# An attention-and-filter kernel on Trainium2: the filter's half-row products on VectorE, output sums partly from PSUM, and another list of batches

## The chip, the cores and the metric

One core of one Trainium2 chip runs the kernel. The metric is the device time of one execution in microseconds (us). Before the change three runs gave a median of 650.92 us (650.14 to 651.53).

The engines are named as in the profile: PE is TensorE's matrix product, PEld its weight load, DVE is VectorE, ACT is ScalarE, POOL is GpSimd, SP is SyncE, which here only issues DMA transfers. SBUF is the on-chip memory; PSUM is the small memory into which PE writes, in 8 banks of 128 partitions by 512 float32 numbers.

## The reference

Two unrelated parts share one launch, and their outputs stand side by side:

```python
S, D, H = 2048, 448, 16; Dh = D // H          # Dh = 28
# A: attention, 16 query heads, one head of keys and values
q = (x @ wq) as 16 heads;  k = x @ wk;  v = x @ wv
p = softmax(q @ k.T * Dh ** -0.5)
a = concat_heads(p @ v) @ wo                   # 2048 x 448
# B: a filter in the frequency domain
X = rfft2(x);  X = X * (w_r + 1j * w_i);  b = irfft2(X)   # 2048 x 448
out = concatenate([a, b], axis=-1)
```

The inputs are float32. The kernel splits an operand into a rounded part and a remainder where it needs float32 accuracy from a faster product: a cast (high part) and a subtraction (low part), both on DVE, and three products instead of one (`mm3`).

## The kernel before

**Attention.** Queries are cut into 4 blocks of 512 (c) and 4 groups of 4 heads (g): 16 pairs (c, g). Keys are cut into 16 blocks of 128. A *step* is one pair and one key block, 256 steps in all. In a step PE makes four score tiles of 128 x 512 (one for each head of the group, L875), each in a bank of its own; their exponentials go to SBUF; PE then multiplies them by the values (L830, eight instructions a step) into a bank that collects 16 steps.

**Batches.** Steps are gathered in batches of two, five or six: first all scores of the batch, then all products with V. The list `PLAN` (L47 to L52) writes each batch as a string. `-` is a score tile whose exponential ACT takes straight from PSUM (L819). `k` is a score tile that DVE copies to SBUF (L881), so that its bank is free early, and that ACT exponentiates later, two tiles in one instruction (L898). `e` is one that ACT takes at once. In batches of five or six the four `k` alternate with the first `-`. The last step of a batch waits in `kept`, and its product with V comes with the next batch. `spread` places the letters of other work among the scores:

- `A` and `B`: the first and second half of a filter unit (`fft2_a`, `fft2_b`), 16 of each,
- `W`: a quarter of the output projection of 128 rows (`wo_unit`), 48 pieces; `X` stands for `WWWW`,
- `Z`: the last stage of the filter (`fft3_a`, then `fft3_b`), 32 pieces; `Y` stands for `ZZ`.

**A filter unit.** `fft2_a(u)` multiplies 128 x 450 numbers by a transform, in three products into one bank (L557 to L559). DVE copies the bank to `us` (L602). POOL makes the two half-row products with the imaginary weights, `p2` from `us` and `wi` (L606, L607: 64 partitions each, crossing halves). DVE makes the product with the real weights, `pf` from `us` and `wr` (L610), splits the next unit's input (L588, L589), then adds the two products (L614) and splits the sum (L615, L616). `fft2_b(u)` multiplies that by the inverse transform, and DVE copies the result out (L628). wr and wi are loaded by DMAs that POOL issues (L575).

**An output quarter.** `fft3_b` makes four products into one bank (L672). DVE copies all of it (L676), then, out of the queue of deferred work, makes a sum and a difference of its halves in SBUF (L690, L683); POOL makes the last sum and difference (L684, L685), and SP stores the result.

**The order of work.** On PE, ACT and DVE the order is written out by the program itself. While it emits PE's instructions it keeps three clocks of planned time (`clock`), one for each engine. `put` queues deferred DVE work with a cost in nanoseconds (one cost for all operations of an entry), `passed` moves PE's clock and pops queued work while DVE's clock is behind, `need` pops until a named entry is done, and `at_once` charges DVE or ACT for work that is emitted on the spot. `take` hands out the bank that is planned to be free first, `give` returns one. `first=True` puts an entry in the queue that is served first. Other deferred DVE work is, for each pair (c, g): the preparation of the next pair's queries (`build_q`, L218, L220, L209, followed by nine DMAs on SP), and the normalisation of a finished pair (`norm`: transposition out of the bank L834, reciprocal L711, division L716, transposition L730, cast L731, subtraction L726, then moves of spare rows by SP and POOL, L700 and L703); and the splits of the slices of wo (`wo_split`, L551 to L554).

## Time and profile before

| | us |
|---|---|
| median of three runs | 650.92 |
| the profiled execution, whole time | 651.21 |
| the profiled execution, span of its instructions | 649.4 |
| PE busy | 639.5 |
| ACT busy | 552.6 |
| DVE busy | 386.4 |
| POOL busy | 121.1 |

A line of a group in the profile reads: line of the kernel, engine, operation, what it writes <- what it reads, shape, count, then busy time in us, mean duration of one in ns, and the idle time of the engine just before them with what ended it. A line of the timeline reads: start and duration in us, engine, line, operation, tiles, count, and in brackets idle time before it. A row of a table of stretches reads: the stretch in us from the start of the span, its length, busy time of PE, PEld, DVE, ACT and POOL with their counts of instructions, granted TensorE clock, share of the DMA engines, GB/s. Buffer numbers are left out of tile names: `s`, `sx` and `po` are banks.

### The profile page before, as it was taken

What the parts mean: (1) busy time and instruction counts of PE and PEld (TensorE: products, weight loads), DVE (VectorE), ACT (ScalarE), POOL (GpSimd) and SP (SyncE); (2) the same over time, 40 slices, a digit from 0 to 9 for tenths busy, and PEclk for the clock granted to TensorE, in tenths of its full rate; (3) what the DMA queues carried; (4) which work ended last, traced back from release to release, by engine and by line L of the source; (5) the groups of instructions that cost most, each with busy time, mean ns of one, the idle gap of its engine ahead of it and who ended that gap; (6) DMA issues with size and microseconds to landing.
All of it is one profiled execution on the core that took longest, in us unless ns stands there. A gap on an engine that the chain in (4) does not pass through costs nothing.

```text
span 649.4 us, 12044 instructions
## 1 busy us (share of the span) xinstructions
PE 639.5 (98%) x4470; PEld 381.7 (59%) x4470; DVE 386.4 (59%) x663; ACT 552.6 (85%) x1013; POOL 121.1 (19%) x182
## 2 busy tenths in 40 slices
PE   8999999999999999999999999999999999999996
PEld 6877655555454665556655565556655665556555
DVE  5999639999898957543753623164636422363631
ACT  5554999998989989888999898989998988989981
POOL 3022304344534221201130200003021100010110
PEclk9999999999999999999999999999999999999999
DMA  8765952443836251315042313013141403040001
GB/s 278 256 165 167 270 131 76 123 124 98 210 78 153 64 130 56 88 32 149 21 114 75 83 46 94 16 47 101 41 131 47 98 15 95 28 100 12 30 31 60
DMA packets 36114, 63.83 MB, mean 98 GB/s; under 512 B 7905, under 2 KB 23922, under 8 KB 35084
## 3 DMA queue, kind: packets, MB, share of 16 engines
q1 hardware_dynamic: 30832, 49.60, 27.7%
q0 software_dynamic: 4640, 12.48, 7.3%
q8 instruction: 36, 0.59, 0.4%
q10 hardware_dynamic: 576, 0.92, 0.4%
q14 instruction: 30, 0.25, 0.1%
HBM read 30.04 MB, written 14.75 MB: 69 GB/s over the span
## 4 chain that ended last, share of the span: by engine, by line
PE 90%; DVE 7%; DMA 1%; ACT 1%; issue 1%; SPq 0%; ACTq 0%; DVEq 0%
PE s L875 28%; PE s L830 22%; PE po L830 6%; PE s L343 6%; PE sx L875 4%; PE po L875 4%; PE s L739 3%; PE sx L830 3%; PE s L141 2%; PE s L672 2%; PE s L658 1%; PE sx L739 1%; PE po L739 1%; DVE bh L588 1%; PE pbb L160 1%; DVE k L881 1%
## 5 line engine op out<-in xcount | busy, mean ns | idle before, releaser
L819 ACT ACTIVATE p<-s 128x512 f32<-128x512 f32 x645 | 344.6, 631 | 40.4 <-PE s L875 33.4
L875 PE MATMUL s<-qa,ka 128*128 128x512 f32 x786 | 238.3, 408 | 2.1 <-DVE k L881 2.1
L875 PEld LDWEIGHTS s<-qa,ka 128*128 128x128 f32 x786 | 144.4, 188 | 76.3 <-issue 30.5
L830 PE MATMUL s<-p,vs 128*32 128x512 f32 x1136 | 134.1, 595 | 0.0
L881 DVE COPY k<-s 128x512 f32<-128x512 f32 x122 | 78.1, 680 | 75.9 <-PE s L875 75.7
L898 ACT ACTIVATE k<-k 128x1024 f32<-128x1024 f32 x86 | 88.1, 1103 | 0.0
L830 PEld LDWEIGHTS s<-p,vs 128*32 128x32 f32 x1136 | 34.4, 109 | 75.1 <-issue 72.2
L819 ACT ACTIVATE p<-sx 128x512 f32<-128x512 f32 x95 | 59.9, 630 | 4.1 <-PE sx L875 3.1
L819 ACT ACTIVATE p<-po 128x512 f32<-128x512 f32 x88 | 55.8, 634 | 6.4 <-PE po L875 4.7
L875 PE MATMUL sx<-qa,ka 128*128 128x512 f32 x121 | 48.8, 403 | 0.0
L703 POOL DMA_DIRECT2D ol<-ol x36 | 18.1, 510 | 161.7 <-DVE ol L726 72.8
L875 PE MATMUL po<-qa,ka 128*128 128x512 f32 x117 | 47.4, 405 | 0.0
L606 POOL TENSOR_TENSOR pwi<-us,wi 64x450 f32<-64x450 f32 x16 | 23.2, 1448 | 113.3 <-DVE us L602 76.3
L881 DVE COPY k<-po 128x512 f32<-128x512 f32 x27 | 18.4, 681 | 41.2 <-PE po L875 41.2
L830 PE MATMUL po<-p,vs 128*32 128x512 f32 x312 | 37.2, 595 | 0.0
L684 POOL TENSOR_TENSOR yo<-y 128x226 f32<-128x226 f32 x16 | 9.8, 610 | 145.5 <-DVE y L683 72.3
L830 PE MATMUL s<-k,vs 128*32 128x512 f32 x272 | 35.6, 594 | 0.0
L834 DVE STREAM_TRANSPOSE osb<-s 128x512 f32<-128x512 f32 x11 | 7.9, 715 | 38.8 <-PE s L830 38.8
L875 PEld LDWEIGHTS po<-qa,ka 128*128 128x128 f32 x117 | 22.0, 188 | 10.2 <-issue 3.4
L875 PEld LDWEIGHTS sx<-qa,ka 128*128 128x128 f32 x121 | 22.7, 188 | 8.3 <-issue 3.4
L830 PE MATMUL sx<-p,vs 128*32 128x512 f32 x208 | 24.8, 595 | 0.0
L881 DVE COPY k<-sx 128x512 f32<-128x512 f32 x23 | 15.6, 680 | 14.1 <-PE sx L875 14.0
(220 smaller groups left out, 841.1 us busy)
## 6 DMA issues: line engine op xcount, KB each, us to landing
qa<-qa SPq DMA_DIRECT2D x15, 512.0 KB
raw<-xa SPq DMA_DIRECT2D x16, 256.0 KB
xb<-xb SPq DMA_DIRECT2D x8, 512.0 KB
qa<-qh SPq DMA_DIRECT2D x64, 64.0 KB
qa<-ql SPq DMA_DIRECT2D x60, 64.0 KB
ob<-yo SPq DMA_DIRECT2D x16, 226.0 KB
t<-bs SPq DMA_DIRECT2D x16, 225.0 KB
wr<-wr POOLq DMA_DIRECT2D x16, 225.0 KB, 5.1
```

The source lines that it names most:

```text
L141: mm(pa[r0:r0 + 32, e, o0:o0 + n], f[:, 2 * r + k, 2 * p + e, h], cs1[:, 2 * r + k, :n], start=True, stop=True)
L343: mm(pq, w[:, j, gs], x[:, j], start=(j == 0 and n == 0), stop=(j == 3 and n == 1))
L606: nc.gpsimd.tensor_tensor(p2[0:64], us[64:128], wi[64:128], op=ALU.mult)
L672: mm(py[:, k], z[:w, r, js], cs3[:w, k], start=True, stop=True)
L684: nc.gpsimd.tensor_tensor(yo[:, 0:2], y1[:, 0], y1[:, 1], op=ALU.add)
L703: nc.gpsimd.dma_start(ol[c][o, g].bitcast(F32), ol[c][r, 0].bitcast(F32))
L739: mm(p, x[c][:, g, s], w, start=(g == 0 and n == 0), stop=(g == NG - 1 and n == 2))
L819: nc.scalar.activation(tiles[-1][:, h % 2], sc, AF.Exp, scale=SCALE)
L830: mm(po[c, g][32 * i:32 * i + 32], vs[:, kc], ps[i // 2][:, i % 2], start=(n == 1), stop=(n == 16))
L875: begun.append(mm(sc, ka[:, kc * 128:(kc + 1) * 128], qa[c, g][:, h], start=True, stop=True))
L881: nc.vector.tensor_copy(keep[h // 2][:, h % 2], sc)
L898: nc.scalar.activation(p, p, AF.Exp, scale=SCALE)
```

## The change

- `fft2_a`: the copy to `us` goes. DVE makes all three products straight from the bank, the two half-row products first. The sum and its split (`pr`) are queued ahead of the next unit's split, which followed the real product before.
- `fft3_b`: DVE copies half of the bank's columns and makes the sum and the difference from the other half in PSUM and this copy, at once; POOL's two operations and the store follow without a queue.
- The list of batches: until step 65 it is the same. Then units A and B stay in batches of five for longer, the four pieces of a projection always stand together (`X`), some together with A and B (`BAX`, `XBB`), and a plain batch of five precedes the first Z. It has 50 batches instead of 49, and 176 tiles `k` instead of 172.
- `put` takes a cost for each operation. The loads and splits of wo are placed anew.

```diff
--- before.py
+++ after.py
@@ -45,11 +45,10 @@
 
 
 PLAN = ["eeeeF", "eeee"] + 4 * [spread(2, "", 0)]
-PLAN += ["-k-k-k-k----------A--"] + [spread(5, u) for u in ["A"] + 9 * ["BA"]]
-PLAN += [spread(6, u) for u in ["BA"] + 4 * ["WBWA"] + 2 * ["WBW"] + ["X"]]
-PLAN += [spread(6, u) for u in 5 * ["Y"] + 4 * ["X"] + 6 * ["Y"] + 4 * ["X"]]
-left = (256 - sum(k in "-ke" for b in PLAN for k in b) // 4)
-PLAN += [spread(6, "Y")] * (left // 6) + [spread(left % 6, "Y")] * (left % 6 > 0)
+FIVE, SIX = spread(5, "BA"), {u: spread(6, u) for u in ("X", "Y", "BAX", "XBB")}
+PLAN += [spread(5, "A", 4, 1.6), spread(5, "A")] + 11 * [FIVE] + [SIX["X"], FIVE, SIX["X"], SIX["BAX"], FIVE]
+PLAN += [SIX["XBB"], spread(5, "")]
+PLAN += 4 * [SIX["Y"]] + 4 * [SIX["X"]] + 7 * [SIX["Y"]] + 4 * [SIX["X"]] + 3 * [SIX["Y"]] + 2 * [spread(5, "Y")]
 
 
 WARM = 10, 10
@@ -215,12 +214,12 @@
                     behind(mv, stored[-1])
             nc.sync.dma_start(q[64:128].bitcast(F32), q[0:64].bitcast(F32))
 
-        ops = [lambda: nc.vector.tensor_scalar(qt, qraw[:, g, cs], mask, cvec[:, g, c:c + 1],
-                                               op0=ALU.mult, op1=ALU.add),
-               lambda: nc.vector.tensor_copy(qh, qt), split]
+        ops = [(540, lambda: nc.vector.tensor_scalar(qt, qraw[:, g, cs], mask, cvec[:, g, c:c + 1],
+                                                     op0=ALU.mult, op1=ALU.add)),
+               (450, lambda: nc.vector.tensor_copy(qh, qt)), (710, split)]
         if not first:
             return ops
-        for op in ops:
+        for _, op in ops:
             op()
         return q, qh, ql
 
@@ -506,11 +505,11 @@
     ap = pools.enter_context(tc.tile_pool(name="ap", bufs=2))
     pp = pools.enter_context(tc.tile_pool(name="pp", bufs=P_BUFS))
 
-    queue, done = (deque(), deque()), {("y", -1), ("pr", -1)}
-
-    def put(key, ops, work=528, first=False):
-
-        for i, op in enumerate(ops):
+    queue, done = (deque(), deque()), {("pr", -1)}
+
+    def put(key, ops, first=False):
+
+        for i, (work, op) in enumerate(ops):
             queue[not first].append(((key if i + 1 == len(ops) else None), op, work))
 
     def pop():
@@ -548,10 +547,10 @@
     def wo_split(g):
         w = wo[g]
         if g >= NG:
-            put(("wo", g), [lambda: nc.vector.tensor_copy(wox[:, g - NG], w)])
+            put(("wo", g), [(400, lambda: nc.vector.tensor_copy(wox[:, g - NG], w))])
             return
-        put(("wo", g), [lambda: nc.vector.tensor_copy(woh[:, g], w),
-                        lambda: nc.vector.tensor_tensor(wol[:, g], w, woh[:, g].bitcast(F32), op=ALU.subtract)])
+        put(("wo", g), [(400, lambda: nc.vector.tensor_copy(woh[:, g], w)), (630, lambda: nc.vector.tensor_tensor(
+            wol[:, g], w, woh[:, g].bitcast(F32), op=ALU.subtract))])
 
     def mm3(out, w, h, l):
         mm(out, fc[w + "h"], h, start=True, stop=False)
@@ -585,8 +584,8 @@
         b = b2["b", q][:, 2 * v:2 * v + 2]
         bh = b2["h", u] = fp.tile([128, 2, DF], F32R, name="bh", bufs=1)
         put(("split", u), [
-            lambda: nc.vector.tensor_copy(bh, b.bitcast(F32)),
-            lambda: nc.vector.tensor_tensor(b, b.bitcast(F32), bh.bitcast(F32), op=ALU.subtract)], first=True)
+            (400, lambda: nc.vector.tensor_copy(bh, b.bitcast(F32))),
+            (630, lambda: nc.vector.tensor_tensor(b, b.bitcast(F32), bh.bitcast(F32), op=ALU.subtract))], True)
 
     def fft2_a(u):
         q, v = divmod(u, 2)
@@ -598,22 +597,20 @@
         pu = halves2(bank)
         mm3(pu, "g1", b2["h", u], b)
         passed(608)
-        us = fp.tile([128, 2, DF], F32, name="us", tag="us", bufs=1)
-        nc.vector.tensor_copy(us, pu)
-        at_once(600)
+        pf, p2 = fp.tile([128, 2, DF], F32, name="pwr"), fp.tile([128, 2, DF], F32, name="pwi")
+        nc.vector.tensor_tensor(p2[0:64], pu[64:128], wi[64:128], op=ALU.mult)
+        nc.vector.tensor_tensor(p2[64:128], pu[0:64], wi[0:64], op=ALU.mult)
+        nc.vector.tensor_tensor(pf, pu, wr, op=ALU.mult)
+        at_once(1800)
         give(bank)
-        pf, p2 = fp.tile([128, 2, DF], F32, name="pwr"), fp.tile([128, 2, DF], F32, name="pwi")
-        nc.gpsimd.tensor_tensor(p2[0:64], us[64:128], wi[64:128], op=ALU.mult)
-        nc.gpsimd.tensor_tensor(p2[64:128], us[0:64], wi[0:64], op=ALU.mult)
         h = fp.tile([128, 2, DF], F32R, name="ph")
         p = fp.tile([128, 2, DF], F32R, name="pl")
-        put(("half", u), [lambda: nc.vector.tensor_tensor(pf, us, wr, op=ALU.mult)], first=True)
+        put(("pr", u), [
+            (700, lambda: nc.vector.scalar_tensor_tensor(pf, p2, sgn, pf, op0=ALU.mult, op1=ALU.add)),
+            (420, lambda: nc.vector.tensor_copy(h, pf)),
+            (640, lambda: nc.vector.tensor_tensor(p, pf, h.bitcast(F32), op=ALU.subtract))], True)
         if u < 15:
             fft2_split(u + 1)
-        put(("pr", u), [
-            lambda: nc.vector.scalar_tensor_tensor(pf, p2, sgn, pf, op0=ALU.mult, op1=ALU.add),
-            lambda: nc.vector.tensor_copy(h, pf),
-            lambda: nc.vector.tensor_tensor(p, pf, h.bitcast(F32), op=ALU.subtract)], first=True)
         pr[u] = h, p
 
     def fft2_b(u):
@@ -671,23 +668,18 @@
         for k, (z, w, r) in enumerate(((ze, 113, 0), (zo, 112, 0), (zo, 112, 1), (ze, 113, 1))):
             mm(py[:, k], z[:w, r, js], cs3[:w, k], start=True, stop=True)
         passed(888)
-        need(("y", 2 * q + v - 1))
-        m = fp.tile([128, 4, 113], F32, name="m", tag="us", bufs=1)
-        nc.vector.tensor_copy(m, py)
-        at_once()
+        y1 = fp.tile([128, 2, 2, 113], F32, name="y1", tag="pwr")
+        m = fp.tile([128, 2, 113], F32, name="m", tag="us", bufs=1)
+        nc.vector.tensor_copy(m, py[:, 2:4])
+        nc.vector.tensor_tensor(y1[:, :, 0], py[:, 0:2], m, op=ALU.add)
+        nc.vector.tensor_tensor(y1[:, :, 1], py[:, 0:2], m, op=ALU.subtract)
+        at_once(1100)
         give(bank)
-        y1 = fp.tile([128, 2, 2, 113], F32, name="y1", tag="pwr")
         yo = fp.tile([128, 4, 113], F32, name="yo", tag="pwi")
-
-        def sums():
-            nc.vector.tensor_tensor(y1[:, :, 1], m[:, 0:2], m[:, 2:4], op=ALU.subtract)
-            nc.gpsimd.tensor_tensor(yo[:, 0:2], y1[:, 0], y1[:, 1], op=ALU.add)
-            nc.gpsimd.tensor_tensor(yo[:, 2:4], y1[:, 0], y1[:, 1], op=ALU.subtract)
-            r0 = (2 * q + v) * 128
-            nc.sync.dma_start(t["ob"][r0:r0 + 128], yo)
-
-        put(("y", 2 * q + v), [
-            lambda: nc.vector.tensor_tensor(y1[:, :, 0], m[:, 0:2], m[:, 2:4], op=ALU.add), sums], 300)
+        nc.gpsimd.tensor_tensor(yo[:, 0:2], y1[:, 0], y1[:, 1], op=ALU.add)
+        nc.gpsimd.tensor_tensor(yo[:, 2:4], y1[:, 0], y1[:, 1], op=ALU.subtract)
+        r0 = (2 * q + v) * 128
+        nc.sync.dma_start(t["ob"][r0:r0 + 128], yo)
 
 
     oh, ol, osb = {}, {}, {}
@@ -727,8 +719,8 @@
             if c < NC - 1:
                 spares(c, g)
 
-        put(("o", c, g), [lambda: divide(c, g), lambda: nc.vector.transpose(o, o),
-                          lambda: nc.vector.tensor_copy(h, o), rest], 640)
+        put(("o", c, g), [(960, lambda: divide(c, g)), (710, lambda: nc.vector.transpose(o, o)),
+                          (430, lambda: nc.vector.tensor_copy(h, o)), (690, rest)])
 
     def wo_mm(p, c, k, gs):
         s = slice(k * 128, k * 128 + 128)
@@ -793,8 +785,8 @@
         if u % 2 == 0 and u < 14:
             at(step - 1, fft2_load, u // 2 + 1)
     for g in range(2 * NG - 1):
-        at(where["B"][g + 2] - 6, wo_load, g)
-        at(where["B"][g + 2], wo_split, g)
+        at(where["B"][g + 1] - 4, wo_load, g)
+        at(where["B"][g + 1] + 4, wo_split, g)
     for q in range(8):
         at(max(where["Z"][4 * q] - 8, where["B"][-1] + 1), fft3_load, q)
 
@@ -847,7 +839,7 @@
         for f, a in later.pop(step, []):
             f(*a)
         if step % 16 == 3 and step < 240:
-            put(("q", step // 16 + 1), build_q(*order[step // 16 + 1]), first=True)
+            put(("q", step // 16 + 1), build_q(*order[step // 16 + 1]), True)
         while norms and step > waits_for_output(norms[0][0]):
             norm(*norms.popleft())
```

## The prediction

> **What bounds the kernel now.** I read the page first, then a table of stretches by batch, then the timeline of VectorE inside two batches.
>
> ```profile
> span 649.4 us, 12044 instructions
> PE 639.5 (98%) x4470; PEld 381.7 (59%) x4470; DVE 386.4 (59%) x663; ACT 552.6 (85%) x1013; POOL 121.1 (19%) x182
> PE 90%; DVE 7%; DMA 1%; ACT 1%; issue 1%; SPq 0%; ACTq 0%; DVEq 0%
> ```
>
> TensorE (PE) sets the time, and the change takes no product from it. What can move is the time in which PE waits. The chain of waits goes through VectorE (DVE) for 7% although DVE is busy 59% of the span: DVE must be late in one stage. The next table shows which. The edges of its stretches are the starts of the products with V (L830) of consecutive batches, as the timeline has them, so each row but the second is one batch of five steps (the first holds one filter unit, the others two) (columns: stretch, its length, busy time of PE, PEld, DVE, ACT, POOL, then clock and DMA). The second row is nine batches in one.
>
> ```profile
> 96.31:106.34 10.03, 10.03 (x64) 5.44 (x64) 9.39 (x14) 9.48 (x19) 4.37 (x4) 1.00 0.08 20
> 106.34:206.71 100.37, 97.43 (x596) 53.51 (x595) 91.59 (x146) 90.30 (x164) 41.18 (x54) 1.00 0.54 138
> 128.50:139.15 10.65, 10.65 (x68) 6.00 (x67) 9.20 (x15) 9.95 (x20) 5.09 (x8) 1.00 0.74 197
> 139.15:150.97 11.82, 10.96 (x67) 5.84 (x66) 11.58 (x19) 9.97 (x20) 3.28 (x4) 1.00 0.16 56
> 173.08:184.01 10.93, 10.91 (x67) 5.92 (x66) 10.67 (x18) 10.04 (x20) 5.08 (x8) 1.00 0.56 151
> 184.01:196.06 12.05, 10.91 (x67) 5.93 (x67) 11.48 (x19) 10.01 (x20) 5.57 (x8) 1.00 0.37 81
> ```
>
> Batches of the same work take 10.65 to 12.05 us, and the long ones are those in which DVE is full (11.58 of 11.82, 11.48 of 12.05). Nine at the shortest length would be 9 x 10.65 = 95.85 us, so 100.37 - 95.85 = 4.52 us are waits. ACT has 9.95 of 10.65 and isn't the limit. The shortest and the longest batch differ so:
>
> ```profile
> 127.38 0.63 DVE L602 COPY us<-s 128x450 f32<-128x450 f32 x1 [0.95 <-PE s L559]
> ...
> 133.70 1.29 DVE L881 COPY k<-s 128x512 f32<-128x512 f32 x2 [0.92 <-PE s L875]
> ```
> ```profile
> 182.90 0.63 DVE L602 COPY us<-s 128x450 f32<-128x450 f32 x1
> 183.44 0.68 DVE L209 TENSOR_TENSOR ql<-ql,qh 128x512 fp32r<-128x512 f32 x1
> 184.04 1.58 DVE L610 TENSOR_TENSOR pwr<-us,wr 128x450 f32<-128x450 f32 x1
> 185.55 1.34 DVE L588 CAST bh<-b 128x450 fp32r<-128x450 f32 x1
> 186.93 0.63 DVE L589 TENSOR_TENSOR b<-b,bh 128x450 fp32r<-128x450 f32 x1
> 187.47 0.68 DVE L614 SCALAR_TENSOR_TENSOR pwr<-pwi,sgn,pwr 128x450 f32<-128x450 f32 x1
> 188.19 0.40 DVE L615 CAST ph<-pwr 128x450 fp32r<-128x450 f32 x1
> 188.62 0.63 DVE L616 TENSOR_TENSOR pl<-pwr,ph 128x450 fp32r<-128x450 f32 x1
> 189.16 0.70 DVE L730 STREAM_TRANSPOSE osb<-osb 128x512 f32<-128x512 f32 x1
> 189.90 0.43 DVE L731 CAST oh<-osb 128x512 fp32r<-128x512 f32 x1
> 190.36 0.69 DVE L726 TENSOR_TENSOR ol<-osb,oh 128x512 fp32r<-128x512 f32 x1
> 190.97 0.68 DVE L881 COPY k<-s 128x512 f32<-128x512 f32 x1
> ...
> 192.17 1.28 DVE L881 COPY k<-s 128x512 f32<-128x512 f32 x2
> ```
> ```profile
> 191.71 0.50 PE L875 MATMUL s<-qa,ka 128*128 128x512 f32 x1 [1.14 <-DVE k L881]
> ```
>
> From the copy that empties the filter's bank (us) to the next score copy (k) pass 6.32 us in the short batch, where k then waits for PE itself (0.92 us idle), and 190.97 - 182.90 = 8.07 us in the long one, where PE waits for k. The long batch is 12.05 - 10.65 = 1.40 us over, so about 8.07 - 1.40 = **6.67 us is what PE gives DVE** between these points; what DVE needs beyond is lost. The durations add up to 8.4 us for the 8.07 us (neighbours overlap a little), so a sum of durations is slightly too high.
>
> **The filter's products (lines 601 to 617).** Two copies of the same kind stand in that list at very different prices: L588 1.34 us, L615 0.40 us, both 128x450 casts. The groups over the nine batches say why:
>
> ```profile
> L588 DVE CAST bh<-b 128x450 fp32r<-128x450 f32 x9 | 10.4, 1159 | 0.0
> L589 DVE TENSOR_TENSOR b<-b,bh 128x450 fp32r<-128x450 f32 x9 | 10.0, 1106 | 0.3
> L610 DVE TENSOR_TENSOR pwr<-us,wr 128x450 f32<-128x450 f32 x9 | 7.4, 821 | 0.2
> L606 POOL TENSOR_TENSOR pwi<-us,wi 64x450 f32<-64x450 f32 x10 | 14.6, 1463 | 50.1 <-DVE us L602 43.3 <-DMA b<-t 6.8
> L607 POOL TENSOR_TENSOR pwi<-us,wi 64x450 f32<-64x450 f32 x9 | 10.3, 1150 | 0.6
> ```
>
> After us, POOL multiplies the two half-rows for 1.46 + 1.15 = 2.6 us, and just then DVE runs L610, L588 and L589, which stretch from 0.63, 0.40 and 0.63 (the shortest row of the same shape in the list above) to 0.82, 1.16 and 1.11. Before, a unit costs DVE 0.63 (us) + 0.82 + 1.16 + 1.11 + 0.68 + 0.40 + 0.63 = 5.43 us. After, there is no us and POOL multiplies nothing in this stage, so the rest returns to its undisturbed price: three products + 0.40 + 0.63 + 0.68 + 0.40 + 0.63 = three products + 2.74.
>
> No row shows a two-operand product that reads PSUM. Below, it can't beat the 0.40 us of the plain cast from SBUF; above I take the 1.16 us of the disturbed cast. Nearest are the copy out of PSUM of the same 450 columns (us, 0.63) and the two-operand L616 (0.63); the half-row products have half the partitions but all 450 columns. I take 0.63, so 1.89 + 2.74 = 4.63 us, 0.8 us less than before.
>
> In the changed program the order on DVE between these products and the next k copy holds, beside those 4.63 us, at most: L209, the transposition and the cast of an output (0.68 + 0.70 + 0.43, together 6.44 us); transposition, cast and subtraction (1.82, 6.45); or the splits of two slices of wo (each a cast and a subtraction like L615 and L616, 2 x 1.03, 6.69 us). All of the eleven groups up to step 75 are at or under the 6.67 us. So nearly the whole 4.52 us go; I keep 0.3 for uneven edges: **-4.2 us**.
>
> [...]
>
> What is moved with it: the bank is held for three products instead of one copy, 1.3 us more. In the changed order its next taker is a score of the following batch, behind all products with V, so these cover it; were the cover gone, a score would wait up to 1.3 us in each batch. A product that waits for wr or wi now stops DVE and the k copies behind it; the loads are issued ten steps ahead, and on POOL's queue nothing but DMA issues stands before them. The q moves on SP keep their place, 13 steps before use.
>
> **The output quarters (fft3_b) and the stores.**
>
> ```profile
> L676 DVE COPY m<-s 128x452 f32<-128x452 f32 x11 | 6.9, 628 | 3.4 <-PE s L672 2.6
> L690 DVE TENSOR_TENSOR y<-m 128x226 f32<-128x226 f32 x16 | 8.1, 505 | 1.2
> ```
>
> Before: a copy (0.63) and two sums at up to 0.51. After: a copy of half the columns (between 0.31 and 0.63) and two sums straight from PSUM at about 0.5, so 1.3 to 1.6 us for 1.65, but all three hold the bank. It is next taken five scores later or more, and DVE is half idle in this stage (rows below): nothing, against up to 0.7 us for each of 16 quarters if the bank were wanted at once. The sums on POOL and the store on SP are now issued at once; behind the store on SP stand q moves and the next quarter's loads, needed a batch later.
>
> **The list of batches.** From the end of the nine batches to the last products with V:
>
> ```profile
> 206.71:628.32 421.61, 421.61 (x2717) 245.52 (x2716) 211.66 (x357) 381.28 (x702) 54.12 (x84) 1.00 0.25 66
> 206.71:300.08 93.37, 93.37 (x567) 53.33 (x566) 61.85 (x94) 83.42 (x155) 19.24 (x20) 1.00 0.29 75
> 339.27:352.18 12.91, 12.91 (x90) 7.63 (x89) 3.93 (x7) 11.96 (x24) 1.65 (x3) 1.00 0.36 98
> 352.18:365.65 13.47, 13.47 (x89) 7.63 (x88) 9.11 (x17) 12.48 (x25) 1.10 (x3) 1.00 0.14 34
> 391.98:405.40 13.42, 13.42 (x84) 7.90 (x83) 3.82 (x6) 11.99 (x24) 0.00 (x0) 1.00 0.41 96
> 616.33:628.32 11.99, 11.99 (x85) 6.92 (x84) 4.82 (x9) 10.54 (x21) 1.08 (x2) 1.00 0.01 1
> ```
>
> Prices of whole batches without waits: five steps with A and B 10.65; with one filter unit 10.03, so a unit is 0.62 and five plain steps 9.41; six steps with four projection pieces (X) 13.42, so BAX and XBB are 13.42 + 1.24 = 14.66; six with two Z (Y) 12.91. The last row is a five behind a six, and so holds one more step of products with V than a five of its own; such a step of eight instructions takes 0.86 us from start to start:
>
> ```profile
> 353.06 1.04 PE L830 MATMUL s<-k,vs 128*32 128x512 f32 x8
> 353.92 1.04 PE L830 MATMUL s<-p,vs 128*32 128x512 f32 x8
> ```
>
> A five with two Z is thus 11.13. From step 65 on, after: 4 x 10.65 + 2 x 13.42 + 2 x 14.66 + 9.41 + 14 x 12.91 + 8 x 13.42 + 2 x 11.13 = **418.6 us** for the same 191 steps, against 421.61: **-3.0 us**. It holds one batch more than before (50 for 49 in all), which costs its change to and from the products with V. What it saves: the 0.56 us of the batch at 352.18 (DVE does an output's division before its k copies there, and two later batches start at the same place in their 16 steps; in the new list none does), and the waits of the stretch to 300.08, in which a projection's bank stays taken over two batches; in one piece it is held for four pieces only. I keep 0.7 back: the first X needs spare rows that are moved only just before it, and the plain five gives ACT no rest.
>
> **Sum.** -4.2 - 3.0 + 0.7 = -6.5 us. The profiled execution took 651.21 us around its span of 649.4; the median of the three runs is 650.92, 0.3 lower. 651.21 - 6.5 = 644.7, from the median 644.4; I say **644.6 us**. Start-up, first filter unit and the final projections are unchanged.
>
> **The rivals.** (1) *The products from PSUM are dear.* At 1.16 us each, the disturbed cast's price, a unit is 3.48 + 2.74 = 6.22 us; with up to 2.06 of other work the groups overrun 6.67 by 0.3 to 1.6 us, by my count 11 us in twelve batches: 650.9 + 11 - 4.5 - 3.0 = 654.4, slower. It decides from about 1.05 us per product. For it: an unseen operation, and twice the reads of PSUM. Against: both nearest rows say 0.63. (2) *DVE stays late in this stage*, since the planner fills the room it has won with other work (the q parts, the splits of wo) ahead of k: then the list alone pays, 650.9 - 3.0 = 647.9. Against it stands the order of the changed program. (3) *The list is no gain*: X in one piece, with its six or more waits for an output's rows, gives back 3 us: 650.9 - 4.2 = 646.7. (4) *Nothing arrives*: (2) and (3) together, 650.9; the waits then come from somewhere that neither part touches, such as ACT at 9.95 of 10.65.
>
> **Chances.** Forecast (643 to 646.5) 0.62; (3) 0.12; (2) 0.10; (4) 0.05; (1) 0.11. The likeliest's own range is 643.2 to 646.5: the lower end is no waits at all (650.9 - 7.5 = 643.4), the upper products of 0.82 us (L610), which cost the fullest groups 1.8 us. The 8-in-10 range is 643.0 to 650.0: it leaves out (1) and most of (4). A change under 0.2% (1.3 us) can't be told from none here. Faster 0.84, same 0.05, slower 0.11.
>
> **What would show it.** Right: every five-step batch between 96 and 210 us at 10.6 to 10.8 us; L588's successor at 0.40 us and L589's at 0.63; three products near 0.63; no idle time of PE put down to a k copy; no batch of Y over 13.1. Wrong: products over 0.9 us; k copies still late with DVE full; PE waiting in the first X batch for oh; more idle time of PE behind ACT in the batches of five.

## The result, and the profile after

The kernel after takes 646.94 us in the median of four runs (646.39 to 647.73), the kernel before 651.2 beside it: ratio 0.9938, 95% interval 0.9921 to 0.9956. In five more runs it took 646.62 (0.9937, 0.9923 to 0.995). The profiled execution took 646.39 us. Its page (span, busy time of the engines, the chain that ended last by engine):

```profile
span 644.5 us, 12021 instructions
PE 639.0 (99%) x4470; PEld 381.5 (59%) x4470; DVE 370.6 (58%) x683; ACT 552.6 (86%) x1011; POOL 79.9 (12%) x150
PE 96%; DMA 1%; DVE 1%; SPq 1%; issue 0%; ACT 0%; ACTq 0%; DVEq 0%
```

PE has 96% of the chain that ended last instead of 90, DVE 1% instead of 7: the late k copies are gone. The view of who waited for whom shows the same. These are the waits that it lists for PE between the batches of two and the tail, first before, then after (us in total, times, longest):

```profile
PE s L875 <- DVE k L881: 2.1, 3, 1.1
PE s L557 <- DVE k L881: 0.9, 1, 0.9
```
```profile
PE s L867 <- DMA qa<-qa: 0.2, 1, 0.2
```

The groups of DVE over the nine batches of five show what the products cost now:

```profile
L609 DVE SCALAR_TENSOR_TENSOR pwr<-pwi,sgn,pwr 128x450 f32<-128x450 f32 x9 | 6.2, 687 | 0.2
L588 DVE TENSOR_TENSOR b<-b,bh 128x450 fp32r<-128x450 f32 x9 | 5.6, 623 | 0.3
L601 DVE TENSOR_TENSOR pwi<-s,wi 64x450 f32<-64x450 f32 x8 | 5.0, 629 | 3.6 <-PE s L558 1.8 <-ACT p L811 1.7
L602 DVE TENSOR_TENSOR pwi<-s,wi 64x450 f32<-64x450 f32 x8 | 5.0, 621 | 0.2
L603 DVE TENSOR_TENSOR pwr<-s,wr 128x450 f32<-128x450 f32 x7 | 4.4, 627 | 0.1
L587 DVE CAST bh<-b 128x450 fp32r<-128x450 f32 x9 | 3.5, 390 | 0.0
```

Products 0.62 to 0.63 us, the cast 0.39 for 1.16, the subtraction 0.62 for 1.11.

For the time by stage I cut each span at the starts of products with V: at the last batch of two, at the batch of steps 60 to 64 (the end of the nine fives), and at the last batch. Stretch M1 lies between the first two, M2 between the last two, T from there to the end of the span. Ahead of M1 no code is changed; its length was 88.44 us in the profile of before, 87.01 and 87.37 in the two of after, and 87.3 to 88.2 in the others, and the order of instructions on DVE and ACT is the same there, so that 1.4 us of the difference of the two spans (4.9) belong to the execution and not to the change. A batch *loses* what it takes beyond the time of its own work on PE.

| kernel | median us | ratio, 95% interval | M1 | M2 | T |
|---|---|---|---|---|---|
| before | 650.7 to 651.2 | | 118.27 | 421.62 | 21.11 |
| after | 646.94 | 0.9938 (0.9921 to 0.9956) | 115.15 | 422.33 | 20.04 |
| after again (r1_again) | 646.62 | 0.9937 (0.9923 to 0.995) | 114.80 | 422.45 | 20.03 |
| e1_products_alone | 649.21 | 0.9974 (0.9962 to 0.9985) | 114.86 | 423.49 | 21.21 |
| e2_old_quarters | 647.62 | 0.9949 (0.9935 to 0.9962) | 114.86 | 423.18 | 20.02 |
| e3_old_list | 648.02 | 0.9954 (0.9941 to 0.9968) | 114.80 | 422.15 | 21.13 |
| e4_list_alone | 651.2 | 1.0005 (0.9996 to 1.0015) | 118.33 | 423.22 | 20.04 |
| e5_idle_products | 647.6, one run | | 115.60 | 422.76 | 20.03 |
| e6_copy_first | 651.53, one run | | 114.42 | 426.35 | 21.17 |
| e7_two_more_on_act | 646.73 | 0.9938 (0.9921 to 0.9954) | 114.79 | 422.06 | 20.02 |
| e8_third_list | 647.38 | 0.9943 (0.993 to 0.9956) | 114.80 | 420.73 | 21.89 |
| e9_q_earlier | 645.89 | 0.9925 (0.991 to 0.994) | 115.08 | 421.25 | 20.02 |
| e10_flat_costs | 647.78 | 0.9947 (0.9935 to 0.9959) | 116.83 | 421.84 | 20.01 |
| e11_together | 647.75 | 0.995 (0.9936 to 0.9964) | 115.09 | 419.78 | 22.95 |

M1 fell by 3.1 to 3.5 us, M2 rose by 0.7 to 0.8, T fell by 1.1. M1 and T repeat to 0.4 and 0.1 us where nothing in them differs, M2 to about 0.4. (e8 and e11 end with a batch of six: 0.86 us, a step of products with V, has moved from M2 to T.) The stretches that matter, after (the second row is the nine batches of five, the fourth is M2):

```profile
94.91:105.42 10.51, 10.51 (x65) 5.43 (x64) 8.83 (x16) 9.94 (x19) 0.11 (x1) 1.00 0.00 1
105.42:202.16 96.74, 96.64 (x595) 54.00 (x595) 85.04 (x154) 89.43 (x164) 18.22 (x35) 1.00 0.56 143
202.16:624.49 422.33, 422.13 (x2717) 245.27 (x2716) 204.01 (x368) 381.39 (x700) 39.75 (x73) 1.00 0.25 66
223.37:236.65 13.28, 13.08 (x76) 7.68 (x76) 7.06 (x13) 11.54 (x23) 2.00 (x4) 1.00 0.39 99
248.02:260.59 12.57, 12.57 (x76) 7.67 (x75) 8.10 (x15) 11.60 (x23) 0.59 (x1) 1.00 0.30 82
301.18:312.07 10.89, 10.89 (x70) 5.09 (x69) 5.55 (x10) 9.45 (x19) 3.15 (x6) 1.00 0.48 136
337.31:350.19 12.88, 12.88 (x89) 7.61 (x88) 3.87 (x6) 11.94 (x24) 0.49 (x1) 1.00 0.26 76
350.19:363.36 13.17, 13.17 (x89) 7.49 (x89) 8.30 (x18) 12.23 (x24) 1.74 (x4) 1.00 0.22 55
```

The nine fives take 96.74 us (96.39 in the second profile) for 100.37. The batch ahead of them takes 10.51 for 10.03. Further on, two batches of the same work (six steps with X) take 13.28 and 12.57, two of Y 13.17 and 12.88. Below, a batch is named by its first step: the 13.28 is batch 75, the 10.51 batch 15.

### The profile page after: what moved, and what is told of

Read it like the earlier page. It is cut to its first block, busy times and chain, and to the rows that moved or that the text cites. A ratio compares the mean times of both kernels' runs of the same rounds, so it can differ in the third digit from the quotient of the medians.

```text
span 644.5 us, 12021 instructions
## 1 busy us (share of the span) xinstructions
PE 639.0 (99%) x4470; PEld 381.5 (59%) x4470; DVE 370.6 (58%) x683; ACT 552.6 (86%) x1011; POOL 79.9 (12%) x150
## 4 chain that ended last, share of the span: by engine, by line
PE 96%; DMA 1%; DVE 1%; SPq 1%; issue 0%; ACT 0%; ACTq 0%; DVEq 0%
PE s L867 30%; PE s L822 23%; PE po L822 7%; PE s L342 6%; PE sx L867 5%; PE sx L822 4%; PE po L867 4%; PE s L731 4%; PE s L140 2%; PE s L655 2%; PE s L669 2%; PE po L731 1%; PE pbb L159 1%; DMA qa<-qa 1%; PE s L290 1%; PE s L558 1%
## 5 line engine op out<-in xcount | busy, mean ns | idle before, releaser
L811 ACT ACTIVATE p<-s 128x512 f32<-128x512 f32 x632 | 340.1, 627 | 37.1 <-PE s L867 31.4
L873 DVE COPY k<-s 128x512 f32<-128x512 f32 x131 | 84.1, 683 | 125.4 <-PE s L867 125.4
L890 ACT ACTIVATE k<-k 128x1024 f32<-128x1024 f32 x88 | 90.3, 1108 | 0.0
L811 ACT ACTIVATE p<-sx 128x512 f32<-128x512 f32 x109 | 68.3, 626 | 7.0 <-PE sx L867 6.4
L811 ACT ACTIVATE p<-po 128x512 f32<-128x512 f32 x83 | 52.8, 636 | 4.8 <-PE po L867 2.3
L867 PE MATMUL sx<-qa,ka 128*128 128x512 f32 x130 | 53.2, 409 | 0.0
L867 PE MATMUL po<-qa,ka 128*128 128x512 f32 x112 | 45.2, 403 | 0.0
L822 PE MATMUL s<-k,vs 128*32 128x512 f32 x296 | 38.7, 594 | 0.0
L867 PEld LDWEIGHTS po<-qa,ka 128*128 128x128 f32 x112 | 21.1, 188 | 7.6 <-issue 2.5
L822 PEld LDWEIGHTS po<-p,vs 128*32 128x32 f32 x328 | 9.8, 110 | 21.9 <-issue 21.3
L342 PE MATMUL s<-xh,wqh 128*128 128x512 f32 x56 | 22.7, 404 | 0.0
```

Source lines behind the costliest of these rows:

```text
L342: mm(pq, w[:, j, gs], x[:, j], start=(j == 0 and n == 0), stop=(j == 3 and n == 1))
L811: nc.scalar.activation(tiles[-1][:, h % 2], sc, AF.Exp, scale=SCALE)
L822: mm(po[c, g][32 * i:32 * i + 32], vs[:, kc], ps[i // 2][:, i % 2], start=(n == 1), stop=(n == 16))
L867: begun.append(mm(sc, ka[:, kc * 128:(kc + 1) * 128], qa[c, g][:, h], start=True, stop=True))
L873: nc.vector.tensor_copy(keep[h // 2][:, h % 2], sc)
L890: nc.scalar.activation(p, p, AF.Exp, scale=SCALE)
```

## The experiments

**The parts alone.** Four kernels, each with one or two parts of the change: r1_again is the kernel after once more. e3_old_list takes back the list and the due steps of wo; e2_old_quarters takes back `fft3_b`; e1_products_alone takes back both, so that `fft2_a` and the costs for each operation are left:

```diff
# e3 and e1, from after
-PLAN += [spread(5, "A", 4, 1.6), spread(5, "A")] + 11 * [FIVE] + [SIX["X"], FIVE, SIX["X"], SIX["BAX"], FIVE]
...
+PLAN += ["-k-k-k-k----------A--"] + [spread(5, u) for u in ["A"] + 9 * ["BA"]]
...
-        at(where["B"][g + 1] - 4, wo_load, g)
-        at(where["B"][g + 1] + 4, wo_split, g)
+        at(where["B"][g + 2] - 6, wo_load, g)
+        at(where["B"][g + 2], wo_split, g)
# e2 and e1, from after
-        nc.vector.tensor_copy(m, py[:, 2:4])
-        nc.vector.tensor_tensor(y1[:, :, 0], py[:, 0:2], m, op=ALU.add)
...
+        nc.vector.tensor_copy(m, py)
+        at_once()
...
```

> The changed kernel once more, to separate what belongs to the program from what differs between executions. 'The middle' below is the stretch from the first products with V of the last two-step batch to those of the last batch: 88.44 to 628.32 = 539.88 us before, 87.01 to 624.49 = 537.48 us in the first profile after. If the middle belongs to the program, it is 537.3 to 537.7 again, and only the stretches before and after it (1.43 and 1.07 us shorter in the first profile after) move. The rival: the middle itself varies by a microsecond or more between executions; then single profiles can't divide the change.

> Of the change only the filter's products (all three on VectorE from PSUM, with the costs per operation); the old list of batches and the old output quarters. Theory 1 (the products pay, the list pays nothing): the five-step batches fall to 10.7 us, the middle to 535.6 to 536.4 us, at least as fast as the whole change. Theory 2 (the products and the list each pay part, as forecast): the middle is about 536.3 and the whole change would be faster, which its 537.48 already speaks against. Theory 3 (the shift of work to VectorE only pays in the new list): the middle stays at 539 or more.

> The changed kernel with the old output quarters (whole bank copied, sums from SBUF out of the queue). Theory A (the new quarters cost, because the bank is held for three operations instead of one and VectorE ends later before the next scores): the Y batches with quarters get shorter, the middle by 0.5 to 1.5 us, 536.0 to 537.0. Rival, as forecast (the quarters cost nothing): the middle within 0.3 us of 537.48.

> The changed kernel with the old list of batches and the old places of the loads and splits of wo. Theory 1: no slower than the whole change, middle 536.0 to 537.0. Theory 2: slower than the whole change by up to 3 us, middle 538.5 to 540.5.

Measured: M1 is the same in all four (114.80 to 114.86), so the products with their costs make all of its gain. From before to e1 M2 *grows* by 1.87 us; from e1 to e3 (the quarters) it falls by 1.34; from e3 to after (the list) it rises by 0.2 to 0.3, while T falls by 1.1. With the old quarters the same list takes 0.3 off M2 (e1 to e2), so either way it is within what M2 repeats to. The medians say the same: 1.7 for the products and costs, 1.2 for the quarters, and 1.1 to 1.4 for the list, which is what T gave. So the quarters are worth 0.7 to 1.3 us, the list nothing in the stage for which it was made. Not all of this was expected: M1 and M2 together are 538.35 us in e1, which none of its three theories gave, and 538.04 in e2, more than either of its two allowed. In r1 (537.25) and e3 (536.96, theory 1's stretch) they are as expected.

The quarters show in the batches with an output's division. In the new list these are 132, 180 and 228: they take 13.43, 13.43 and 13.42 us with the old quarters (e2) and 13.17, 13.25 and 13.17 with the new, 0.69 us together, nearly all of the 0.7 to 0.85 that e2 and after differ by in M2. This is the batch at 131 of the old list in e1, then in e3, each with the line of DVE that first takes from the bank of its second quarter:

```profile
349.44:363.34 13.90, 13.90 (x90) 7.51 (x89) 8.74 (x17) 12.60 (x25) 0.70 (x2) 1.00 0.11 29
```
```profile
363.09 0.63 DVE L674 COPY m<-s 128x452 f32<-128x452 f32 x1
```
```profile
349.08:362.49 13.41, 13.41 (x90) 7.51 (x89) 8.08 (x17) 12.11 (x24) 1.74 (x4) 1.00 0.05 15
```
```profile
360.55 0.39 DVE L674 COPY m<-sx 128x226 f32<-128x226 f32 x1
```

The batch is 0.49 us shorter. DVE has 0.66 us less in it, part saved and part moved to the next batch: a quarter costs DVE 1.41 us by the old way (0.63 + 0.39 + 0.39) and 1.17 by the new. The order changes more. The old copy comes after `need` has emptied the queue up to the sums of the quarter before, and here an output's cast and subtraction stand ahead of these sums. So the bank of the second quarter is first read 13.65 us into the batch, by the new way 11.47. That this late bank is what PE lacks is my reading; PE's list names no wait for DVE there.

**The list alone**: before, with the new list and the new due steps of wo.

```diff
-PLAN += ["-k-k-k-k----------A--"] + [spread(5, u) for u in ["A"] + 9 * ["BA"]]
...
+PLAN += [spread(5, "A", 4, 1.6), spread(5, "A")] + 11 * [FIVE] + [SIX["X"], FIVE, SIX["X"], SIX["BAX"], FIVE]
...
```

> The kernel before with nothing but the new list of batches (and the new places of the loads and splits of wo). So far the list was worth nothing in the middle when the products were on VectorE (e3 536.96, whole change 537.25 to 537.48), but the forecast gave it 3 us. Theory L1 (the list only pays where VectorE has room, since it puts four more units into batches of five): the old waits for k copies stay in the batches to step 65 (stretch 8 to 60 at 118.3 us) and come in the four new batches of five too; middle 541 to 543, slower than before's 539.88. Theory L2 (the list pays by itself, and the products on VectorE take it back): middle 536.5 to 538.

Measured: the ratio is 1.0005, no gain. M2 is 1.6 us longer than with the old list, T 1.1 shorter, and the waits for k copies stay (M1 is 118.33 us), as theory L1 has it.

**POOL beside DVE again**: after, with two products on POOL that nobody reads.

```diff
+        junk = fp.tile([128, 2, DF], F32, name="junk", bufs=1)
+        nc.gpsimd.tensor_tensor(junk[0:64], p2[0:64], wi[0:64], op=ALU.mult)
+        nc.gpsimd.tensor_tensor(junk[64:128], p2[64:128], wi[64:128], op=ALU.mult)
```

> The changed kernel, in which POOL makes two more half-row products of the old size, into a tile that nobody reads, right after VectorE's half-row products; the result is unchanged. Theory C (the old casts and subtractions were slow because POOL was multiplying at the same time): operations of VectorE of the same shape that run beside them stretch to 0.8 to 1.3 us from 0.40 and 0.63, the fullest groups pass 6.67 us, and the stretch 8 to 60 (114.8 to 115.2 us after) gets 2 to 6 us longer, with waits of PE for k copies. Rival (the unit got shorter because one pass fewer is made and the order is better, not because POOL stopped): the stretch stays within 0.5 us of 115.

```profile
L612 DVE SCALAR_TENSOR_TENSOR pwr<-pwi,sgn,pwr 128x450 f32<-128x450 f32 x9 | 10.9, 1207 | 0.2
L606 POOL TENSOR_TENSOR junk<-pwi,wi 64x450 f32<-64x450 f32 x9 | 10.0, 1110 | 0.7
L605 POOL TENSOR_TENSOR junk<-pwi,wi 64x450 f32<-64x450 f32 x9 | 9.8, 1089 | 38.7 <-DVE pwi L601 38.5
L208 DVE TENSOR_TENSOR ql<-ql,qh 128x512 fp32r<-128x512 f32 x3 | 2.9, 956 | 0.0
```

That POOL's products made these operations of DVE long is shown: the addition behind the products goes from 0.69 to 1.21 us in the mean, L208 from 0.68 to 0.96, as soon as POOL multiplies beside them. I read it as a wait (see the last section). The price in time is below both the theory's 2 us and the expected waits for k copies: M1 grew by 0.45 to 0.8 us, in one run, and PE has no wait for a k copy. The timeline of DVE goes with that. From the first operation on the filter's bank to the next k copy, where DVE has no rest in between, pass up to 8.08 us in the fives of before and up to 7.02 in e5, in which less other work stands between them at 25, 35, 40 and 55.

**The bank freed by a copy**: e1, with the copy to `us` back and all three products on DVE from SBUF.

```diff
-        nc.vector.tensor_tensor(p2[0:64], pu[64:128], wi[64:128], op=ALU.mult)
...
+        nc.vector.tensor_copy(us, pu)
+        at_once(600)
+        give(bank)
+        nc.vector.tensor_tensor(p2[0:64], us[64:128], wi[64:128], op=ALU.mult)
...
```

> e1 (products alone, old list, old quarters) with the bank copied to us first and the three products made from us on VectorE: POOL still multiplies nothing, the bank is held for one copy instead of three products, and VectorE has one copy of 0.63 us more in each unit. Theory H (the bank held for three products makes PE wait for ACT's banks where no other cover lies behind A): the batches at steps 15, 65, 71 and 83, which lost 0.61, 0.60, 0.70 and 0.69 us in e1, are back at 0.13, 0.10, 0.45 and 0.44, while the fullest five-step batches pass 6.67 us and lose 0.3 to 0.6 each. Rival (those four losses come from the costs in the plan or the order of the sum and the split): they stay as in e1.

Measured: batch 15 takes 10.14 us (10.51 with the bank held), and the timeline of PE at its end says why. After, then e6 (start, duration):

```profile
104.01 0.50 PE L867 MATMUL sx<-qa,ka 128*128 128x512 f32 x1
104.50 0.50 PE L867 MATMUL po<-qa,ka 128*128 128x512 f32 x1
104.99 0.50 PE L867 MATMUL s<-qa,ka 128*128 128x512 f32 x1
```
```profile
104.10 1.58 PE L876 MATMUL s<-qa,ka 128*128 128x512 f32 x5
```

In the first the scores come every 0.49 us, and the weight loads of all three wait 0.3 us for an exponential of ACT: they go at ACT's pace, because one bank is missing, the one that the three products hold. In e6 they start 0.23 to 0.38 us apart (five in 1.58), and the one wait of a weight load is for the copy to `us`. Eight scores of the same batch follow `A` here, five in the usual batch of five. Batch 65 of the old list, with seven scores behind `A`, and batch 83, with four but with a projection's bank taken too, lose 0.5 and 0.26 us less in e6 than in e1. The 0.63 us that a unit costs DVE more did no harm in the fives, against the expectation: M1 is the shortest of all, 114.42. The planner is charged for the copy too, and puts less other work between the bank and the next k copy (in the batch at 45 one subtraction in place of two splits of wo), so that no such group is longer than 6.79 us. The long M2 (426.35) has one late k copy, for which PE waits 2.64 us in the batch at 71. DVE stands before it:

```profile
222.98 0.39 DVE L551 CAST wox<-wo 128x448 fp32r<-128x448 f32 x1 [3.83 <-DMA wo<-wo]
```

The load of this slice of wo was issued only at 219.13, since POOL waited 5.7 us for an earlier L551 to free the slice's buffer. So the work that the planner had put off was what made the k copy late, and e6 says nothing of the batch at 71 itself.

**The tail.** T is 20.0 with the new list and 21.1 with the old, though its code is the same. The new list's program has two instructions fewer on ACT; e7 is after with two tiny ones more at the start:

```diff
+            for _ in range(2):
+                nc.scalar.activation(warm, warm, AF.Copy)
```

> The changed kernel with two tiny instructions more at the start of ACT, beside the warm-up, where ACT waits for data anyway. The three programs with the old list end 21.1 us after the first products with V of their last batch, those with the new list 20.0: after its last branch, over the guarded part, ACT needs 2.4 us to its next instruction in the first kind and 0.45 in the second. Theory F (it depends on where in ACT's instruction stream the branch's target lies, and the new list has two ACT instructions fewer): the stretch from the branch to the next instruction changes to some 2.4 us and the end comes 1.1 us later, 21.1. Rival (it belongs to the list in another way, say to the DMAs under way): the end stays at 20.0.

Measured: T stays at 20.02. The number of ACT's instructions as the page counts them (1013 in before and in e7) isn't the cause.

**A third list, an earlier q, flat costs.** Three kernels, each from after with one edit:

```diff
# e8_third_list
-PLAN += [spread(5, "A", 4, 1.6), spread(5, "A")] + 11 * [FIVE] + [SIX["X"], FIVE, SIX["X"], SIX["BAX"], FIVE]
-PLAN += [SIX["XBB"], spread(5, "")]
+PLAN += [spread(5, "A", 4, 1.6), spread(5, "A")] + 14 * [FIVE] + [SIX["XBB"], SIX["X"]] + 2 * [spread(5, "X")]
...
# e9_q_earlier
-        if step % 16 == 3 and step < 240:
+        if step % 16 == 1 and step < 240:
# e10_flat_costs, in put
+            work = 640 if key[0] == "o" else 528
```

> The kernel after, with one line of the list changed: no plain batch of five at all, the two batches of six that hold filter units come right behind the batches of five, two fives with four projection pieces follow them, and the rest are sixes; 49 batches instead of 50. Theory ACT (the waits that the new list brought sit in the plain five, in the batch of four pieces at step 75 and in the one at 103, where ACT runs short): its plain five (0.75 us lost), the batch at 75 (0.73 to 0.84) and the Y batch at 114 (0.34) have no successors with such losses, and the stretch from step 8 to the last batch falls from 537.3 by 0.8 to 1.5 us, to 535.8 to 536.5; the median is about 645.5. Rival (any list has its own waits of this size, as the old one has them elsewhere): the stretch stays at 537.0 to 537.6, median 646.5 to 647. If fives with four pieces are themselves short of ACT, the stretch is longer than 537.6 and the two new fives lose over 0.5 us each.

> The kernel after, with the next q asked for two steps earlier (at every sixteenth step plus one instead of plus three). Theory (the batch at step 75 waits 0.47 us for the move of q, which is late because its ops stand in a full VectorE queue): the batch at 75 falls from 0.73 to 0.84 us of loss to about 0.3, what remains being ACT's; other batches as they were; the stretch from step 8 to the last batch falls by 0.4 to 0.5 us to about 536.8. Rival (the q ops then push filter ops behind them, and the batches of five lose more): the batches of five go from 0.20 to 0.3 or more each, and the stretch doesn't fall.

> The kernel after, with the planner's costs for queued VectorE operations flat again (640 for an output's operations, 528 for all others), the costs of the operations done at once as they are. Theory (the per-operation costs alone hurt in the late batches with an output's start in them: in the kernel with the products alone the batch at 131 went from 0.64 to 1.06 us of loss, those at 179 and 227 from 0.64 to 0.82): the batches at 132, 180 and 228 lose 0.1 to 0.3 us less each, the stretch from step 60 to the last batch falls by 0.4 to 0.8 us from 422.4. Rival (the products' own cost at once, 1800, or the place of the list is what did it): nothing changes there, within 0.2 us. Second rival: flat costs are too low for a division of about 0.96 us, VectorE runs late, and the stretch gets longer by over 0.5 us.

e8: M1 and M2 together are 535.53 us. With the step that has moved to T (0.86), which the expectation forgot, that is 536.39 against 537.25 and 537.48: 0.9 to 1.1 us gained, the size that theory ACT gave, and no batch from 60 to 124 loses over 0.35 us. The theory isn't shown by that: the loss of batch 75, which the theory put down to ACT, goes with an earlier q too, as e9 shows next. The median doesn't show it, since T went back to the long form (21.89 - 0.86 = 21.03).

e9: right in place, and larger than expected. Batch 75 takes 12.58 us for 13.28 (13.39 in the second profile), and the median is the lowest of all, 645.89. M1 and M2 together are 536.33 us, 0.9 to 1.15 less than after, where 0.4 to 0.5 were expected. Beside batch 75, those at 114 and 162 are 0.28 and 0.24 us shorter, that at 180 is 0.25 longer, and two of the fives lose 0.3 more between them. Batch 75 in e9, and its first two scores in after:

```profile
223.60:236.18 12.58, 12.58 (x76) 7.65 (x76) 7.06 (x13) 11.40 (x23) 2.00 (x4) 1.00 0.32 84
```
```profile
227.80 0.50 PE L867 MATMUL s<-qa,ka 128*128 128x512 f32 x1
228.50 0.47 PE L867 MATMUL s<-qa,ka 128*128 128x512 f32 x1 [0.20 <-DMA qa<-qa]
```

The second score of the batch starts 0.70 us after the first, behind the move of q. The four k tiles at the head of a batch belong to its *last* step; batch 75 ends with step 80, the first of a pair, so it wants the new q when step 75 begins, 8 steps after it was asked for at step 67, and not 13. The ACT waits that I had put beside it (0.26 us) went too.

e10: M2 falls by 0.5 to 0.6 us as its theory has it, but not where it says: the batches at 132, 180 and 228 lose 0.31, 0.31 and 0.50 for 0.33, 0.42 and 0.34. What falls is 0.14 to 0.29 each in five others (103, 114, 162, 198, 216). And M1 grows by 1.7 to 2.0, since q comes late in the batch at 60:

```profile
198.87 0.70 PE L868 MATMUL s<-qa,ka 128*128 128x512 f32 x2 [1.80 <-DMA qa<-qa]
```

So the costs for each operation keep q in time there, and are worth more than they cost. They have a small part in e1's longer M2: the batch at 197 (198 in the new list) takes 12.94 to 12.96 us in the three kernels with flat costs (before, e4, e10) and 13.12 or 13.13 in the nine others that have it.

**Both, with ACT's program kept short.**

```diff
# from e8, with e9's edit
-        (nc.scalar if on_act else nc.sync).dma_start(t["oa"][r0:r0 + 128], y)
+        nc.sync.dma_start(t["oa"][r0:r0 + 128], y)
...
-        wo_out(p, c, k, True)
+        wo_out(p, c, k, k % 2 > 0)
```

> The third list and the earlier q together, and at the very end all four of the last outputs stored from SP, two of them copied out by DVE instead of ACT. This leaves ACT 1280 instructions and semaphore steps, against 1288 with the third list alone. Theory COUNT (the time from ACT's last branch to its next step is long, 2.4 us, in the programs in which ACT's records number 1288 to 1300, and short, 0.45 us, in those with 1277 to 1282): it is 0.45 us here, and the tail is 20.9 us where the third list alone had 21.9 (its last batch is a six, which adds one step's 0.86 to the tail and takes it from the middle). Rival (the list decides, or the number of batches: 49 batches are long, 50 are short): it is 2.4 us and the tail 21.7 to 21.9. The middle, from step 8 to the last batch: 534.9 to 535.7 if the earlier q adds something to the third list's 535.53 (its batches at 130 and 136 lose 0.64 and 0.68), over 535.8 if q ahead of the filter's operations costs more than it brings there. Median 645.0 to 646.0 by COUNT, 646.3 to 647.4 by its rival.

M2 is the shortest (419.78; 420.64 with the moved step, 1.7 to 1.8 under after's), M1 and M2 together (534.87) are as expected, and the batches at 130 and 136 lose 0.17 and 0.22 for 0.64 and 0.68 in e8. T is the longest. The last branch of the program (it jumps over code that runs only for large inputs) and the next step behind it on the same engine, with start times in us, in before, after and e11:

```profile
L943 ACTq COMPARE_BRANCH  x1: 54/54/54, 646.0 to 646.0; - x1
L943 ACTq EVENT_SEMAPHORE  x1: 17/17/17, 648.5 to 648.5; - x1
```
```profile
L935 ACTq COMPARE_BRANCH  x1: 54/54/54, 642.2 to 642.2; - x1
L935 ACTq EVENT_SEMAPHORE  x1: 17/17/17, 642.6 to 642.6; - x1
```
```profile
L934 SPq EVENT_SEMAPHORE  x5: 17/17/17, 643.9 to 644.2; - x5
...
L934 ACTq COMPARE_BRANCH  x1: 50/50/50, 640.3 to 640.3; - x1
L934 ACTq EVENT_SEMAPHORE  x1: 17/17/17, 640.7 to 640.7; - x1
L934 SPq COMPARE_BRANCH  x1: 50/50/50, 641.3 to 641.3; - x1
```

ACT's jump takes 2.5 us in before and 0.4 in after and in e11: COUNT holds. Its rival falls, since e8 has the same list as e11 and a jump of 2.5 us. (The expectations give the third list 49 batches; it has 50, as after, so the number of batches was no rival any more once e8's jump was long.) But the time was mispredicted under both, since the stores that I moved to SP made SP the last to jump, and SP's jump took 2.6 us (641.3 to 643.9). In the other 13 profiles SP's jump takes 2.7 to 3.0 us, but begins at 625 to 632 us and lies hidden there.

## Why the prediction was right, and where not

The forecast was 644.6 us, the range 643.0 to 650.0; measured were 646.9 and 646.6. Direction and range held; the likeliest case's own range (643.2 to 646.5) was just missed. Of the terms, the products' came out; the quarters' and the list's were wrong, in opposite directions, and 1.1 us of the gain, at the very end, is luck. Of the signs that were named, those on the products and the k copies held. The fives hold with one exception (11.06 us at 60 in the first profile, 10.72 in the second). "No batch of Y over 13.1" failed: five take 13.12 to 13.25 us.

**The filter's products (-4.2): right, 0.2 to 0.6 short in the fives.** Products of 0.63 us, the cast and the subtraction back at 0.39 and 0.62, and nine batches of 96.74 and 96.39 us for the 96.15 of the forecast; e1 shows that this part alone does it. Rivals 1 (dear products) and 2 (DVE stays late) fell. The bound of 6.67 us for a group (from DVE's first operation on the filter's bank to the next k copy) fits the waits that went, to 0.2 us. In before the groups of 25, 35, 40, 45 and 50 are over it by 0.80, 1.39, 0.60, 0.19 and 0.29 us, and these batches take 0.80, 1.18, 0.62, 0.18 and 0.29 us more than 10.65. (It was read off 55; 20, which follows a batch without `B`, doesn't fit.) After, no group in which DVE has no rest is longer than 6.65. (One of the three sums that the prediction calls at or under the bound, 6.69, is over it.)

One thing in the sum was not taken apart. The unit got 0.8 us shorter, but the program also puts less other work into the groups of 25, 35, 40 and 55. In that of 55 a cast and a subtraction of an output (1.12 us) are gone from it. The planner is charged 4.59 us for a unit (1800 + 1760 + 1030 ns) where it was charged 3.77 (600 + 6 x 528), although the unit costs less. With the other work of before the groups of 35 and 55 (8.06 and 8.08 us) would still be some 0.6 us over, so by this estimate about 1.2 of the 4.5 us of waits are the planner's. No run has the new products with the old charge.

What a source in PSUM and the pair of half-row products cost can be read off now. The products from SBUF in e6, and the timeline of DVE in after (start, duration):

```profile
L608 DVE TENSOR_TENSOR pwr<-us,wr 128x450 f32<-128x450 f32 x9 | 5.7, 629 | 0.2
L606 DVE TENSOR_TENSOR pwi<-us,wi 64x450 f32<-64x450 f32 x9 | 5.6, 623 | 0.3
```
```profile
111.23 0.68 DVE L873 COPY k<-sx 128x512 f32<-128x512 f32 x1
111.83 1.28 DVE L873 COPY k<-s 128x512 f32<-128x512 f32 x2
...
115.16 0.63 DVE L601 TENSOR_TENSOR pwi<-po,wi 64x450 f32<-64x450 f32 x1
115.82 0.62 DVE L602 TENSOR_TENSOR pwi<-po,wi 64x450 f32<-64x450 f32 x1
```

The products take no longer from PSUM than from SBUF: 627 ns (L603) and 629 ns (L601) from PSUM, 629 and 623 from SBUF. The two half-row products don't overlap: L602 starts 0.03 us behind the end of L601, where two k copies overlap by 0.08. The time shows no cost of it: the fullest fives, at 45 and 50, take 10.70 and 10.72 us like the others.

**The bank held for three products (nothing): wrong in batch 15.** The step said that the next taker is a score of the following batch. Where more scores of the same batch follow `A` than five, they want the bank: +0.48 us in batch 15, and e6 takes 0.37 of it back. In the old list it also hits the batches at 65 and 83, 0.76 of the 1.87 us by which e1's M2 is longer. That at 71, made like 83, is 0.25 us longer too. The rest lies in later batches, 0.2 of it by the costs, and its cause is open.

**The output quarters (nothing): wrong, they gain.** e1 against e3 gives 1.2 us in the medians, e2 against after 0.7 to 1.0. "DVE is half idle in this stage" was an average over the stage. In the batches in which an output is divided DVE isn't idle when the second quarter comes, and the old quarter stood in the queue behind that work.

**The list (-3.0, with 0.7 kept back): wrong in the stage, made good by chance in the tail.** In M2 it gains nothing (e3 against after), alone it costs 1.6 us (e4). Two steps failed. First, the prices of "whole batches without waits" were taken as the new batches' prices. The plain five, priced at 9.41, takes 10.89 - 0.86 = 10.03 (its edges hold one step more). That is just what a five with one piece took before (10.03), so the first piece cost nothing: the price of a second piece (0.62; the prediction says unit, but `A` and `B` are halves of one) was taken off once too often. Batch 75 waited for q, 0.71 us. Both were named where I kept 0.7 us back, and together they are 0.62 + 0.71 = 1.3 us. XBB, priced at 14.66, takes 14.28 + 0.86 = 15.14, another 0.5 us, which nothing in the prediction named. At the end of the plain five PE's scores fall into ACT's pace: the weight loads of the last three wait 0.30 us each for an exponential (the last three of XBB, too, come 0.49 us apart and wait 0.27 to 0.31):

```profile
309.13 1.34 PE L867 MATMUL s<-qa,ka 128*128 128x512 f32 x5
310.30 0.40 PE L867 MATMUL po<-qa,ka 128*128 128x512 f32 x1
310.66 0.51 PE L867 MATMUL sx<-qa,ka 128*128 128x512 f32 x1
311.15 0.99 PE L867 MATMUL s<-qa,ka 128*128 128x512 f32 x2
```

Five scores in 1.34 us, then steps of 0.36 and 0.49. The claim that the q moves cost nothing "13 steps before use" is the same error: true for steps, not for the k tiles, and e9 shows it. Second, "in the new list none does", of batches in which DVE divides an output ahead of its k copies: the batches at 132, 180 and 228 start one place further in their 16 steps than 131, 179 and 227 did, and lose just as much with the old quarters (0.58 to 0.60 us over their work; 0.33 to 0.42 with the new). The one at 132 has 12.23 us of ACT where a quiet Y has 11.94.

Rival 3, "the list is no gain", gave 646.7 and comes out with that number; the place that it named, an output's rows in X, was not the one. T's 1.1 us were in no step and in no rival: without them after would stand at about 648, where e3 with the old list is.

**Sum as measured**: M1 -3.1 to -3.5, M2 +0.7 to +0.8, T -1.1, together -3.5 to -3.7; the medians differ by 4.3. The rest isn't placed: ahead of M1, where nothing is changed, single executions differ by up to 1.4 us.

## What to carry to other kernels

Price a re-cut batch by the engine that has least room in it, not by PE alone, and ask of every early-issued tile which step it belongs to: what was to be needed "13 steps later" was needed at the head of the batch here, after 8, and cost 0.71 us. The bank held 1.3 us longer wasn't free where its next taker was near (0.48 us in batch 15); look at each place in the schedule at which the unit stands, not at the usual one. And cut the profile at fixed points of the work before crediting a part with a change of the median: here a quarter of the gain was a jump at the very end.

## What the runs showed of the hardware

The jump at the end of ACT's program took about 2.5 us in the five profiles in which ACT's records in the trace (instructions and semaphore steps) number 1288 to 1300 (before 1291, e1, e3, e6, e8), and 0.4 to 0.5 in the nine with 1277 to 1282. e11 was cut to 1280 for this and fell on the short side as forecast. On POOL it took 0.5 us in the 13 profiles with 220 to 269 records and 2.7 in e5, with 284. So on these two engines the long jump goes with the larger number of records; what makes it long, no run here tells. The end comes 1.1 us later for it, and not 2, because in the short case SP is then the last; the first drains of the two in after:

```profile
L1118 SPq DRAIN  x3: 7/7/13, 643.6 to 643.9; - x3
L1118 ACTq DRAIN  x2: 8/8/8, 642.7 to 644.0; - x2
```

In the fives of before, each of these operations of DVE that starts inside a product of POOL ends a fixed time behind the end of that product, which I read as a wait: every such subtraction (L589) 0.48 or 0.49 us behind L607, every such cast (L588) 0.25 or 0.26 behind L606 or L607, both such products (L610) 0.49 behind L606. In e5 the additions do the same: six of the nine start inside a product of POOL and end 0.49 or 0.48 us behind it (1.32 to 1.59 us long), and the three that don't take 0.68 or 0.69, one of them with a product of POOL that starts 0.37 us behind its own start. Not every operation does so: in after, seven of the differences made from the bank (L675) start inside a sum of POOL (L680), take the 0.38 us of the other nine and end 0.01 to 0.03 behind it.
